# Stacked attention scores: one VectorE reduction in place of a ScalarE copy and a VectorE add, and the first parts of the keys made by ScalarE

## The chip, the cores and the metric

The kernel runs on one core of a Trainium2 chip. The metric is the device time of one execution in microseconds (us). Two timed runs of the kernel before gave 1043.73 and 1044.98 us, with a median of 1044.36. About 2% (21 us) of it is what counts as a difference here.

## The reference

The program is a linear attention, and behind it a mixture of experts that takes every token through all four experts. There are 32 heads of width 64 over 576 tokens, and 2304 tokens for the experts:

```
proj = x @ w_phi                      # x = q or k; w_phi is 64 x 128
proj = proj - max(|proj|) per row
phi  = concat(exp(proj), exp(-proj))  # 256 features
num  = phi(q) @ (phi(k).T @ v)
den  = phi(q) @ sum(phi(k)) + 1e-6
x    = num / den                      # heads side by side: 2304 x 512
out  = sum over e of p[:, e] * (relu(x @ w1[e]) @ w2[e])
```

All arrays are fp32. The kernel multiplies in a rounded fp32 format, and where that would cost accuracy it splits an operand into a first part ("hi": the value rounded) and a second part ("lo": the value minus the first part), and adds up products of the parts.

## The kernel before, in words

The attention is worked off in 16 **pairs** of heads, numbered 0 to 15 here. A pair has 576 tokens, laid out as 5 tiles of 128 for the keys (the last one half empty) and 4 tiles for the queries. They are taken in chunks: k 0 and k 1 have two tiles each, k 2 has one; q 0 and q 1 have two each.

From pair 4 on the scores are **stacked** (STACKED = 4). The 64 rows of a head's keys fill 64 partitions with their first parts, and the other 64 partitions hold their second parts; the weights `wst` hold the first parts of `w_phi` in columns 0 to 127 and the second parts in columns 128 to 255. One matmul of 128 x 256 (line 195) then leaves for each token two blocks of 128 columns whose sum is the score. A tile of two heads fills one PSUM tile of 512 columns. `proj_add` (lines 215 to 226) sums the blocks: ScalarE copies the second block from PSUM into the SBUF tile `d` (L225), then VectorE adds the first block to it (L226). `proj_sub` follows on VectorE: the maximum of the absolute values (L236) and its subtraction (L240). Then ScalarE takes the exponentials, TensorE transposes the queries' scores, and products follow.

`split_pair` (lines 165 to 183) makes those parts of the keys (`kst`) and queries (`qst`). `round_to` makes the first part on the engine that the tables HI_ENG0 (pairs 0 to 3) and HI_ENG (pairs 4 to 15) name, by a letter for the keys and one for the queries: v is VectorE (L160), a is ScalarE (L162), g is GpSimd (L158). The second part is always a subtraction on GpSimd (L181).

From pair 4 on the experts' matmuls on the first 512 tokens (L606, L570, `first_units`) are woven into the attention's. The order of everything is written by hand: STAGES gives each step of a pair a due time, 16 steps of a clock after the pair before, and a queue of steps is run down in the order of their due times (`run_until`). So the program order is fixed when the kernel is built, each engine works its own instructions strictly in that order, and they wait for each other only by semaphores. An instruction that waits holds up all that stand behind it on its engine.

Three PSUM tiles (`ps_att`, bufs=3) go round among the scores (`proj`), the transposed queries (`dT`) and the products (`num`). A matmul into such a tile waits until the reader of the tile three before it is through. Of `num`, the copies to `nd` are made by VectorE for the first head of the first 256 columns (L299) and by ScalarE for the rest (L301). They belong to the pair before the one whose keys are just being scored.

Of the kernel before, what the change touches and what calls it, by code (L numbers as in the profile page):

```python
# [13 lines left out]
AF = mybir.ActivationFunctionType  # L14
ALU = mybir.AluOpType
AX = mybir.AxisListType
# [4 lines left out]
def kernel(  # L21
# [16 lines left out]
    nc = tc.nc  # L38
# [3 lines left out]
    NF = w_phi.shape[1]  # L42
# [19 lines left out]


    COPY_ENG, COPY_ENG0 = "vvaaaa", "vaaaaa"
    LO_ENG, LO_ENG0, HI_ENG, HI_ENG0 = "vgg", "vgv", "vg", "ag"

    XA_START, XA_GAP, XA_LATE, XA_LOAD = 11, 0.7, 3.7, 1.5
    FETCH = (12, 28, 40, 46)
# [147 lines left out]
    def proj_add(i, what, c):  # L216

        s = pairs[i]
        if i < STACKED:
            return  # L220
        d = s.d[what, c] = ap_.tile([P, 512], F32, name="d", tag="d", bufs=3)
        for j, ps in enumerate(s.ps.pop((what, c))):
            a = ps.rearrange("p (h s f) -> p h s f", s=2, f=NF)
            dv = d[:, j * 256 : (j + 1) * 256].rearrange("p (h f) -> p h f", f=NF)
            nc.scalar.activation(dv, a[:, :, 1], AF.Copy)  # L225
            nc.vector.tensor_tensor(dv, a[:, :, 0], dv, op=ALU.add)  # L226

    def proj_sub(i, what, c):

# [199 lines left out]
    def x_store(i):  # L429
# [10 lines left out]
        (-7.5, split_pair, ("k",)),  # L440
        (-1.9, split_pair, ("q",)),
        (-0.3, proj, ("k", 0)), (0.1, proj_add, ("k", 0)), (0.6, proj_sub, ("k", 0)), (2.7, k_exp, (0,)),
        (7.2, k_kv, (0,)),
        (2.1, proj, ("k", 1)), (2.1, proj_add, ("k", 1)), (2.1, proj_sub, ("k", 1)), (3.9, k_exp, (1,)),
        (10, k_kv, (1,)),
        (2.8, proj, ("k", 2)), (3.1, proj_add, ("k", 2)), (3.4, proj_sub, ("k", 2)), (8.3, k_exp, (2,)),
        (12.2, k_kv, (2,)), (13, kv_hi, ()), (13.2, kv_lo, ()),
        (5.5, proj, ("q", 0)), (6.0, proj_add, ("q", 0)), (6.4, proj_sub, ("q", 0)), (8.4, q_tr, (0, 0)), (9.4, q_exp, (0, 0)),
# [488 lines left out]
```

## Time and profile before

| | |
|---|---|
| median of the timed runs | 1044.36 us (1043.73 to 1044.98) |
| the profiled execution, its own time | 1045.42 us |
| its span, first to last instruction | 1043.6 us |
| TensorE, matmuls busy | 977.1 us (94%) |
| VectorE busy | 725.0 us (69%) |
| ScalarE busy | 460.6 us (44%) |
| GpSimd busy | 584.8 us (56%) |
| `proj_add` of the stacked pairs runs from | 61.2 us to 396.5 us |

Busy time is the time in which an engine has an instruction under way; overlapping instructions are counted once, so the mean of one instruction times their count can be more than the group's busy time. The views below name engines PE (TensorE), DVE (VectorE), ACT (ScalarE) and POOL (GpSimd). Where an engine was idle ahead of an instruction, square brackets give the idle time and what ended it. A row with x2 or x4 merges so many instructions, and its second number is then the time from the first one's start to the last one's end.

### The profile page before, as it was taken

The page shows a single profiled execution, that of the slowest core. Times are in us where ns is not written, and L with a number is a line of the kernel's source. Part 1 is how long each engine was busy: PE and PEld are TensorE (multiplying, and loading weights), DVE is VectorE, ACT ScalarE, POOL GpSimd, SP SyncE. Part 2 cuts the span into 40 slices and gives each one's busy share as a digit, 9 for nine tenths or more (in the row PEclk, how much of TensorE's full clock was granted, in tenths as well). Part 3 has the DMA queues.
Part 4 walks back from the last instruction along what each step waited for, and adds up shares of the span by engine and source line. Part 5 has one row for each costly group of instructions (what it writes and reads, how often), then busy time and mean ns, then how long its engine had stood idle before and what let it go on. Part 6 is the DMA issues. An engine that isn't in the chain of part 4 may idle for free. (4 is left out here: it accounts for less than half of the span.)

```text
span 1043.6 us, 13596 instructions
## 1 busy us (share of the span) xinstructions
PE 977.1 (94%) x4923; PEld 833.9 (80%) x4923; DVE 725.0 (69%) x1110; ACT 460.6 (44%) x880; POOL 584.8 (56%) x439
## 2 busy tenths in 40 slices
PE   7977888999888889889999999999999999999998
PEld 6867777877777778667888888888878888888887
DVE  5567777776777676687667566666886767767764
ACT  4755554565455554344333333333343443443441
POOL 3645676775655663556445545544565556556551
PEclk9989999999999899999999999999999999999999
DMA  5422323332323213511212221121114122222211
GB/s 149 131 70 66 101 77 87 107 90 72 92 92 94 76 52 96 163 63 61 91 41 71 62 60 40 60 63 41 41 42 162 54 68 74 61 69 73 61 49 61
DMA packets 70610, 80.37 MB, mean 77 GB/s; under 512 B 34160, under 2 KB 36080, under 8 KB 70544
## 3 DMA queue, kind: packets, MB, share of 16 engines
q1 hardware_dynamic: 70544, 79.51, 25.5%
q8 instruction: 39, 0.64, 0.3%
q14 instruction: 27, 0.22, 0.1%
HBM read 72.00 MB, written 7.49 MB: 76 GB/s over the span
## 5 line engine op out<-in xcount | busy, mean ns | idle before, releaser
L580 DVE SCALAR_TENSOR_TENSOR out<-l,pr,out 128x512 f32<-128x512 f32 x270 | 200.4, 747 | 100.2 <-PE l L570 99.0
L570 PE MATMUL l<-w2hi,h_lo 128*128 128x512 f32 x576 | 229.9, 399 | 12.5 <-DVE out L580 12.5
L570 PE MATMUL l<-w2hi,h_hi 128*128 128x512 f32 x576 | 228.6, 397 | 0.0
L570 PE MATMUL l<-w2lo,h_hi 128*128 128x512 f32 x576 | 228.2, 396 | 0.0
L570 PEld LDWEIGHTS l<-w2hi,h_lo 128*128 128x128 f32 x576 | 109.7, 190 | 34.5 <-DVE out L580 17.0
L537 POOL TENSOR_TENSOR w1lo<-wraw,w1hi 128x512 fp32r<-128x512 f32 x64 | 79.7, 1265 | 96.5 <-ACT w1hi L529 58.6
L570 PEld LDWEIGHTS l<-w2hi,h_hi 128*128 128x128 f32 x576 | 109.6, 190 | 23.7
L500 POOL TENSOR_TENSOR w2lo<-wraw,w2hi 128x1024 fp32r<-128x1024 f32 x48 | 116.9, 2436 | 14.9 <-ACT w2hi L494 11.0
L570 PEld LDWEIGHTS l<-w2lo,h_hi 128*128 128x128 f32 x576 | 109.6, 190 | 17.6
L727 ACT ACTIVATE h_hi<-c 128x512 fp32r<-128x512 f32 (+1 forms) x96 | 55.0, 578 | 68.7 <-DVE c L724 67.7
L737 POOL TENSOR_TENSOR c<-u,s 128x512 f32<-128x512 f32 (+1 forms) x32 | 37.5, 1173 | 85.2 <-DVE u L724 85.2
L288 PEld LDWEIGHTS kv<-v,e 128*128 128x128 f32 x640 | 81.9, 200 | 3.7 <-issue 0.4
L181 POOL TENSOR_TENSOR kst<-kq,kst 64x640 fp32r<-64x640 f32 x24 | 42.8, 1783 | 66.2 <-issue 49.7
L288 PE MATMUL kv<-v,e 128*128 128x66 f32 x640 | 79.7, 279 | 0.0
L537 POOL TENSOR_TENSOR s_lo<-ws,s_hi 128x768 fp32r<-128x768 f32 x32 | 59.1, 1848 | 34.9 <-ACT s_hi L529 34.9
L753 ACT ACTIVATE c<-c 128x512 f32<-128x512 f32 (+1 forms) x32 | 18.5, 580 | 123.8 <-POOL c L737 123.8
L226 DVE TENSOR_TENSOR d<-proj,d 128x256 f32<-128x256 f32 x108 | 41.1, 417 | 46.0 <-ACT d L225 45.5
L240 DVE TENSOR_TENSOR d<-d,m 128x512 f32<-128x512 f32 (+1 forms) x60 | 66.5, 1108 | 2.1
L734 POOL TENSOR_TENSOR h_lo<-c,h_hi 128x512 fp32r<-128x512 f32 (+1 forms) x32 | 37.5, 1173 | 40.2 <-ACT h_hi L727 40.2
L494 ACT ACTIVATE w2hi<-wraw 128x1024 fp32r<-128x1024 f32 x48 | 50.6, 1053 | 13.7 <-PE l L570 13.2
L606 PE MATMUL l<-x_hi,w1lo 128*128 128x512 f32 x128 | 53.7, 419 | 0.0
L529 ACT ACTIVATE s_hi<-ws 128x768 fp32r<-128x768 f32 x32 | 27.1, 847 | 59.4 <-DVE ws L513 59.4
(156 smaller groups left out, 2291.3 us busy)
## 6 DMA issues: line engine op xcount, KB each, us to landing
wraw<-in_w_dram SPq DMA_DIRECT2D x96, 512.0 KB
kq<-in_kq_dram SPq DMA_DIRECT2D x31, 256.0 KB
rb<-rec_d SPq DMA_DIRECT2D x32, 144.0 KB
out_dram<-out SPq DMA_DIRECT2D x18, 256.0 KB
v<-in_v_dram SPq DMA_DIRECT2D x32, 128.0 KB
xd<-rb SPq DMA_DIRECT2D x8, 288.0 KB
xr<-xd SPq DMA_DIRECT2D x2, 768.0 KB
kq<-in_kq_dram SPq DMA_DIRECT2D x32, 32.0 KB
```

The lines of the kernel that those rows point to most:

```text
L181: nc.gpsimd.tensor_tensor(st[o, h], raw[r, sl], st[r, h].bitcast(F32), op=ALU.subtract)
L226: nc.vector.tensor_tensor(dv, a[:, :, 0], dv, op=ALU.add)
L240: nc.vector.tensor_tensor(d[:, :n].rearrange("p (g f) -> p g f", f=NF), psv, m[:, :g].unsqueeze(2).to_broadcast([P, g, NF]), op=ALU.subtract,)
L288: nc.tensor.matmul(s.kv[:, n * KW : (n + 1) * KW], lhsT=e[:, e0 : e0 + NF], rhs=s.v[:, t, h * KW : (h + 1) * KW], start=(c == 0 and j == 0 ...
L494: nc.scalar.activation(hi, raw, AF.Copy)
L500: nc.gpsimd.tensor_tensor(lo, raw, hi.bitcast(F32), op=ALU.subtract)
L537: nc.gpsimd.tensor_tensor(dst, src, hi.bitcast(F32), op=ALU.subtract)
L570: nc.tensor.matmul(ps, lhsT=l[:, f, j * P : (j + 1) * P], rhs=r[:, f, :], start=(f == 0 and k == 0), stop=(f == 1 and k == 2),)
L580: nc.vector.scalar_tensor_tensor(o, ps, p, o, op0=ALU.mult, op1=ALU.add)
L606: nc.tensor.matmul(banks[n, f], lhsT=l[:, ksl], rhs=r[:, k, :], start=(k == 0 and j == 0), stop=(k == NP - 1 and j == 2),)
L727: nc.scalar.activation(h[b][0][:, f, :nt], src, AF.Relu)
L734: nc.gpsimd.tensor_tensor(dst, src, hi.bitcast(F32), op=ALU.subtract)
```

## The change

In `proj_add` the copy and the addition give way to one VectorE instruction for each tile: a `tensor_reduce` that reads all 512 columns of the PSUM tile, viewed so that the two addends of a score stand innermost (they lie 128 columns apart), and writes their 256 sums to `d`. ScalarE has no part in it any more. And in HI_ENG the letter for the keys goes from v to a, so that ScalarE makes the first parts of the keys of pairs 4 to 15.

```diff
-    LO_ENG, LO_ENG0, HI_ENG, HI_ENG0 = "vgg", "vgv", "vg", "ag"
+    LO_ENG, LO_ENG0, HI_ENG, HI_ENG0 = "vgg", "vgv", "ag", "ag"
...
         for j, ps in enumerate(s.ps.pop((what, c))):
-            a = ps.rearrange("p (h s f) -> p h s f", s=2, f=NF)
+            a = ps.rearrange("p (h s f) -> p h f s", s=2, f=NF)
             dv = d[:, j * 256 : (j + 1) * 256].rearrange("p (h f) -> p h f", f=NF)
-            nc.scalar.activation(dv, a[:, :, 1], AF.Copy)
-            nc.vector.tensor_tensor(dv, a[:, :, 0], dv, op=ALU.add)
+            nc.vector.tensor_reduce(dv, a, axis=AX.X, op=ALU.add)
```

The changed file is one line shorter, so behind `proj_add` its line numbers are one lower. On TensorE, GpSimd and SyncE the instructions and their order stay as they were. On VectorE, 108 additions become 108 reductions in the same places, and 24 casts go. On ScalarE 108 copies go and 24 casts come.

The first place is VectorE on the keys of pair 9, from the first sum to the copy `nd` that ScalarE's next copies wait for. Before:

```order
L226 TENSOR_TENSOR d<-proj,d 128x256 x2
L236 TENSOR_REDUCE m<-d 128x4
L240 TENSOR_TENSOR d<-d,m 128x512
L580 SCALAR_TENSOR_TENSOR out_86<-l_2087,pr,out_86 128x512
L226 TENSOR_TENSOR d<-proj,d 128x256 x2
L236 TENSOR_REDUCE m<-d 128x4
L240 TENSOR_TENSOR d<-d,m 128x512
L226 TENSOR_TENSOR d<-proj,d 128x256
L236 TENSOR_REDUCE m<-d 128x2
L240 TENSOR_TENSOR d<-d,m 128x256
L299 TENSOR_SCALAR nd<-num,eps 128x256
```

Now:

```order
L225 TENSOR_REDUCE d<-proj 128x256 x2
L235 TENSOR_REDUCE m<-d 128x4
L239 TENSOR_TENSOR d<-d,m 128x512
L579 SCALAR_TENSOR_TENSOR out_86<-l_2040,pr,out_86 128x512
L225 TENSOR_REDUCE d<-proj 128x256 x2
L235 TENSOR_REDUCE m<-d 128x4
L239 TENSOR_TENSOR d<-d,m 128x512
L225 TENSOR_REDUCE d<-proj 128x256
L235 TENSOR_REDUCE m<-d 128x2
L239 TENSOR_TENSOR d<-d,m 128x256
L298 TENSOR_SCALAR nd<-num,eps 128x256
```

The five sums stand where they stood; each is now a reduction of 512 columns that reads PSUM alone.

The second place is ScalarE at the same time, from the last rounding of the exponentials of pair 8 (`ehi`) to its copy `nd`. Before:

```order
L258 ACTIVATE ehi<-e 128x640
L225 ACTIVATE d<-proj 128x256 x4
L494 ACTIVATE w2hi<-wraw 128x1024
L253 ACTIVATE e_2133<-d 128x4x128
L254 ACTIVATE e_2133<-d 128x4x128
L225 ACTIVATE d<-proj 128x256
L301 ACTIVATE nd<-num,eps 128x256
```

Now:

```order
L257 ACTIVATE ehi<-e 128x640
L493 ACTIVATE w2hi<-wraw 128x1024
L252 ACTIVATE e_2084<-d 128x4x128
L253 ACTIVATE e_2084<-d 128x4x128
L300 ACTIVATE nd<-num,eps 128x256
```

The five copies `d`, which stood behind `ehi`, are gone, and VectorE's sums no longer have ScalarE's queue ahead of them.

The third place is the cast of the keys of pair 10, before on VectorE, behind the sums of the last queries of pair 9:

```order
L226 TENSOR_TENSOR d<-proj,d 128x256 x2
L593 SCALAR_TENSOR_TENSOR h_lo<-l_2181,h_hi 128x512
L160 CAST kst<-kq 64x640 x2
L580 SCALAR_TENSOR_TENSOR out_86<-l_2255,pr,out_86 128x512
L236 TENSOR_REDUCE m<-d 128x4
```

and now on ScalarE, behind `h_hi`, ahead of the exponentials of pair 9's first queries:

```order
L622 ACTIVATE h_hi<-l_2131 128x512
L162 ACTIVATE kst<-kq 64x640 x2
L493 ACTIVATE w1hi<-wraw 128x1024
L252 ACTIVATE e<-dT 128x512
L253 ACTIVATE e<-dT 128x512
```

The cast has changed engines, and two instructions of 64 x 640 now stand ahead of `e` on ScalarE.

## Rows read from the trace of the kernel before

**Rows 1.** The page's first part: busy us, share of the span, instructions.

```profile
PE 977.1 (94%) x4923; PEld 833.9 (80%) x4923; DVE 725.0 (69%) x1110; ACT 460.6 (44%) x880; POOL 584.8 (56%) x439
```

**Rows 2.** Stretches of 14 us: length, busy us by engine, clock, DMA; sum.

```profile
200.00:214.00 14.00, 11.95 (x70) 9.99 (x68) 12.14 (x21) 8.99 (x21) 9.41 (x8) 1.00 0.37 108
214.00:228.00 14.00, 14.00 (x88) 12.32 (x87) 10.24 (x16) 7.56 (x16) 10.53 (x8) 1.00 0.24 60
...
sum 336.00, PE 294.74 PEld 251.51 DVE 242.13 ACT 181.20 POOL 206.78; mean PE 12.28 PEld 10.48 DVE 10.09 ACT 7.55 POOL 8.62
```

**Rows 3.** Waits from 60 to 400, TensorE, VectorE: us, times, longest.

```profile
PE proj L195 <- ACT nd L301: 12.0, 9, 2.1
PE proj L195 <- DVE d L226: 11.1, 16, 2.1
PE num L363 <- ACT nd L301: 9.4, 9, 3.2
...
DVE d L226 <- ACT d L225: 45.5, 30, 4.4
```

**Rows 4.** Groups by form, VectorE, ScalarE: count, busy us, mean ns, idle.

```profile
L240 DVE TENSOR_TENSOR d<-d,m 128x512 f32<-128x512 f32 x48 | 59.4, 1237 | 1.7
L226 DVE TENSOR_TENSOR d<-proj,d 128x256 f32<-128x256 f32 x108 | 41.1, 417 | 46.0 <-ACT d L225 45.5 <-PE l L570 0.5
...
L160 DVE CAST kst<-kq 64x640 fp32r<-64x640 f32 x24 | 12.1, 503 | 0.4
L240 DVE TENSOR_TENSOR d<-proj,m 128x512 f32<-128x512 f32 x16 | 11.1, 692 | 1.1
...
L236 DVE TENSOR_REDUCE m<-proj 128x4 f32<-128x512 f32 x16 | 11.0, 689 | 6.7 <-PE proj L211 6.6
...
L236 DVE TENSOR_REDUCE m<-proj 128x2 f32<-128x256 f32 x4 | 1.7, 422 | 0.6 <-PE proj L211 0.6
...
L856 DVE TENSOR_REDUCE prs<-pr 128x18 f32<-128x72 f32 x1 | 0.2, 217 | 0.0
...
L225 ACT ACTIVATE d<-proj 128x256 f32<-128x256 f32 x108 | 36.4, 381 | 21.9 <-PE proj L195 21.7
...
L162 ACT ACTIVATE kst<-kq 128x640 fp32r<-128x640 f32 x3 | 2.2, 737 | 0.1
```

**Rows 5.** VectorE by time, pair 9: start, us, line, idle before, releaser.

```profile
200.14 0.75 DVE L580 SCALAR_TENSOR_TENSOR out<-l,pr,out 128x512 f32<-128x512 f32 x1 [0.43 <-PE l L570]
201.21 0.76 DVE L226 TENSOR_TENSOR d<-proj,d 128x256 f32<-128x256 f32 x2 [0.32 <-ACT d L225]
...
208.47 0.48 DVE L299 TENSOR_SCALAR nd<-num,eps 128x256 f32<-128x256 f32 x1
```

**Rows 6.** ScalarE in order of time, pair 9.

```profile
208.98 0.47 ACT L301 ACTIVATE nd<-num,eps 128x256 f32<-128x256 f32 x1 [3.19 <-DVE nd L299]
```

**Rows 7.** TensorE in order of time, pair 9.

```profile
198.77 0.64 PE L195 MATMUL proj<-wst,kst 128*128 128x256 f32 x4
...
209.50 0.51 PE L195 MATMUL proj<-wst,qst 128*128 128x256 f32 x2 [0.96 <-ACT nd L301]
```

**Rows 8.** VectorE in order of time, pair 10.

```profile
226.73 0.21 DVE L393 RECIPROCAL rec<-den 128x9 f32<-128x9 f32 x1
229.25 0.76 DVE L226 TENSOR_TENSOR d<-proj,d 128x256 f32<-128x256 f32 x2 [2.31 <-ACT d L225]
...
236.60 0.47 DVE L299 TENSOR_SCALAR nd<-num,eps 128x256 f32<-128x256 f32 x1
```

**Rows 9.** TensorE in order of time, pair 10.

```profile
225.86 0.63 PE L195 MATMUL proj<-wst,kst 128*128 128x256 f32 x4
...
229.73 0.50 PE L195 MATMUL proj<-wst,kst 128*128 128x256 f32 x2 [0.93 <-DVE d L226]
...
237.63 0.50 PE L195 MATMUL proj<-wst,qst 128*128 128x256 f32 x2 [1.50 <-ACT nd L301]
```

**Rows 10.** GpSimd in order of time, ahead of pair 10.

```profile
218.60 3.44 POOL L181 TENSOR_TENSOR kst<-kq,kst 64x640 fp32r<-64x640 f32 x2 [3.17 <-issue]
```

## The prediction

> **What bounds the kernel now.** I start from the page's busy times: TensorE has matmuls under way in 94% of the span [rows 1], so a change can give back only time in which TensorE waits. The change touches the stretch of the stacked pairs, some 336 us of the span, so the next view is the engines' busy time there in stretches of 14 us. A pair takes about two of them, and they alternate [rows 2]: in the half in which a pair's keys are scored (200 to 214 us) VectorE is busy for 12.14 us of 14 and TensorE leaves 2.05 us idle; in the other half (214 to 228) TensorE has no gap and VectorE has 3.8 us to spare. Over the 336 us TensorE is idle for 336 - 294.74 = 41.3 us. The view of the waits says for what [rows 3]: 11.1 us for the additions of `proj_add` to give a PSUM tile back, 12.0 + 9.4 us for ScalarE's copies `nd`. Both hang on VectorE: the ScalarE copy of pair 9 at 208.98 sat idle for 3.19 us for VectorE's own `nd` [rows 6], which stands at the end of the VectorE chain of the keys' scores, at 208.47 [rows 5], and TensorE's next scores waited 0.96 us for that [rows 7]. So the question is when that chain starts and how long it is. The same view shows what may shorten it: VectorE sat for 45.5 us, in 30 waits, ahead of its additions until ScalarE's copies came [rows 3].
>
> **The change, part by part.**
>
> *The sums.* 108 additions of 417 ns and 108 copies of 381 ns [rows 4] go; 108 reductions of 512 columns come. No row shows such a reduction (pairs of columns 128 apart, from PSUM). The nearest is the maximum over 512 columns of a PSUM tile, 689 ns, and 422 ns over 256 [rows 4]: 267 ns for 256 columns, 1.04 ns a column. A penalty for many small groups would show in L856, with 18 groups of four: by the same slope 72 columns should take 422 - 184 x 1.04 = 230 ns, and it took 217 [rows 4]. Going by columns read, I take 689 ns, so +272 ns for each tile and +29.4 us of VectorE work in all. The lower end is the addition's 417 ns, if the work went by sums written; the upper end is a second read time for each column, 689 + 512 x 1.04 = 1222 ns, since every row here reads columns that lie side by side and excludes no price for a jump. I take the value near the lower end because rows of the same operation, from the same memory, with as many columns, give it.
>
> [...]
>
> *The casts.* 24 casts of 503 ns leave VectorE, -12.1 us [rows 4]. They stand behind the last queries' sums, in the half where VectorE has slack, so I count nothing for it. On ScalarE I take 737 ns, from its three casts of 640 columns on 128 partitions [rows 4], some +17.7 us against -36.4 us for the copies that go; it is busy for 7.56 us of that half's 14 [rows 2], which hides the casts. Behind the cast hangs GpSimd's subtraction `kst`: in pair 10 it ran from 218.60 to 222.04, after 3.17 us of idle time [rows 10], and TensorE first read it at 225.86 [rows 9]. That is 3.8 us of cover, against two casts of 1.5 us together; the cast may also come earlier, as it no longer stands behind a VectorE queue. SyncE's and GpSimd's orders do not change, no DMA is moved, and the new wait of the reductions, for a free `d`, falls on readers that are done before the scores come.
>
> *The start of the chain.* Without the copy, the first sum waits only for TensorE and for VectorE itself. Pair 9 is the worst case. TensorE was through with the two tiles at 198.77 + 0.64 = 199.41 [rows 7], VectorE came free at 200.14 + 0.75 = 200.89, and the additions began at 201.21 [rows 5]: 0.32 us are won. Pair 10 is the good case: scores done at 226.49 [rows 9], VectorE free at 226.94, additions at 229.25 [rows 8]: 2.30 us are won.
>
> *The length of the chain.* Two additions take 0.76 us [rows 5], two reductions by the same overlap 2 x 0.689 - 0.07 = 1.31: +0.55. The keys have two chunks of two tiles and one of one: +0.55 + 0.55 + 0.27 = +1.37 us up to `nd`.
>
> *The sum.* In pair 9 `nd` comes 1.37 - 0.32 = 1.05 us later, and TensorE, which waited for it, loses 1.05 us. In pair 10 it comes 2.30 - 1.37 = 0.93 us earlier; TensorE, which waited 0.93 us for the first sum and 1.50 us for `nd` [rows 9], can use it. What the second half does to it is nothing: TensorE is full there. The queries' sums gain by the missing copy about what they lose (two reductions after the scores instead of copy, then two additions). Twelve pairs between these ends give -11.2 to +12.6 us. The idle time ahead of all additions, 45.5 us [rows 3], against 29.4 us more work says that good and bad cases are mixed; I take the middle, +0.06 us a pair, +0.7 us in all. So the change moves 29 us onto an engine that is nearly full where it counts and takes away a handoff that cost it as much: **no difference that can be measured**. The profiled execution took 1045.42 us (span 1043.6 and 1.8 around it), 1.06 above the median of the timed runs. 1045.4 + 0.7 is 1046.1, by the median 1045.1; I say 1046.
>
> **The rivals.**
>
> *Slower: the jump is paid.* If a column that does not lie beside the last one costs a second read time, the reduction takes 1222 ns. The five tiles of the keys then add 5 x 0.533 = 2.67 us to the chain, so TensorE loses 3.7 us in pair 9 and 1.7 us in pair 10, 2.7 in the middle, 33 us for twelve pairs: 1079 us. It decides at about 0.34 us more than 689 ns a tile (5 x 12 x 0.34 = 21 us). [...] Against it: the row of 689 ns reads one column in 1.04 ns and shows no sign of the memory being the limit, but it reads side by side. Chance 0.19.
>
> *Faster: the chain also gets shorter.* The subtraction L240 takes 1237 ns where both operands are in SBUF and 692 ns where one is in PSUM [rows 4]; GpSimd works beside it for 8.62 us of every 14 [rows 2]. If ScalarE's earlier casts let GpSimd run its `kst` in its 3.17 us of idle time [rows 10], less of its work falls on the chain. If that wins half of the 0.545 us on two subtractions a pair, 12 x 2 x 0.27 = 6.5 us come off: 1039 us. With pair 10's case in most pairs besides (-11 us) it is 1028, and only with all the 0.545 us on top under 1024. Against it: GpSimd's next steps wait for ScalarE's exponentials of the pair, which do not come earlier. Chance 0.14, of which 0.05 below 1023.
>
> *The cast comes late.* If ScalarE reaches the cast so late that GpSimd's `kst` ends after 225.86, TensorE loses what goes over 3.8 us, in each pair; 2 us over would be 24 us, 1070. ScalarE stands idle for 6.4 us of that half, so I give it 0.02.
>
> That the change doesn't do what it says is excluded by the program order: the 108 reductions and the casts stand where the text puts them.
>
> **How the numbers follow.** The forecast, no measurable difference, has 0.65 and its own range is 1034 to 1058, the two ends of the sum. The faster rival has 0.14, the paid jump 0.19, the late cast 0.02. Two per cent, about what a measurement of this kernel can tell from no change, are 21 us: 1023.5 and 1065.2. Below lies 0.05. Above lie the paid jump and the late cast with 0.20, some of it nearer and some beyond 1079. Within lies 0.75. A range of 1032 to 1077 holds the forecast's own range (about 0.6 of all cases), two thirds of the faster rival and under half of the slower ones, some 0.8 together.
>
> **What would show it.** In the profile of the changed kernel the group of the reductions should read 690 ns; 950 or more means the paid jump, under 500 that it goes by sums written. VectorE's idle time for ScalarE ahead of the sums should be gone, and in its place stand waits for TensorE's scores. The chain from the first sum of pair 9 to its `nd`, 7.26 us before [rows 5], should take 8.6. TensorE's waits for the sums should stay near 11 us and those for `nd` near 21; if these fall to half, the faster rival is at work. ScalarE's casts should take 740 ns, and TensorE's waits for `kst` should stay small beside these. The prediction is wrong if the stretch of the stacked pairs changes its length by more than 13 us, whatever the reductions take.

## The result, and the profile after

Two timed runs of the changed kernel gave 1031.02 and 1032.16 us, a median of **1031.59 us** against 1044.36: a ratio of 0.9878 (95% interval 0.9835 to 0.9920). Six later executions gave 0.9843 (0.9811 to 0.9875). So it is some 13 to 16 us faster: a gain that is clear of the noise, and smaller than the 2% that the prediction set as the bound. The forecast was 1046 us; the time lies 0.4 us below the range of 1032 to 1077.

The profiled execution took 1031.02 us, its span is 1029.2 us and the mean granted clock of TensorE 0.986 (before: 1043.6 us, 0.976). The page's first part, which answers to [rows 1]:

```profile
PE 966.5 (94%) x4923; PEld 825.1 (80%) x4923; DVE 737.1 (72%) x1086; ACT 446.0 (43%) x796; POOL 575.2 (56%) x439
```

TensorE runs the same 4923 matmuls, but has them under way for 10.6 us less. Its idle time (span less busy time) went from 1043.6 - 977.1 = 66.5 us to 1029.2 - 966.5 = 62.7 us, by 3.8. So of 14.4 us of span about three quarters came from matmuls that ran faster, and one quarter from waits.

The groups by form, VectorE and ScalarE (count, busy us, mean ns, idle time before), which answer to [rows 4]:

```profile
L225 DVE TENSOR_REDUCE d<-proj 128x256 f32<-128x512 f32 x108 | 69.4, 678 | 7.7 <-PE proj L195 5.4 <-ACT kst L162 2.0
L239 DVE TENSOR_TENSOR d<-d,m 128x512 f32<-128x512 f32 x48 | 56.8, 1184 | 1.7
...
L235 DVE TENSOR_REDUCE m<-d 128x4 f32<-128x512 f32 x48 | 32.8, 683 | 1.2
...
L162 ACT ACTIVATE kst<-kq 64x640 fp32r<-64x640 f32 x24 | 17.7, 736 | 0.6
```

The reduction takes 678 ns, as the 689 of the forecast had it, and no more than the 683 ns of L235, which reads 512 columns that lie side by side in SBUF (688 ns where L235 reads PSUM): the jump of 128 columns cost nothing here. The casts took 736 ns (737 forecast). The 45.5 us in which VectorE sat idle for ScalarE's copies are gone; 2.0 us of waits for ScalarE's cast `kst` have come. But the subtraction, which the change did not touch, went from 1237 to 1184 ns.

The waits from 60 to 400 us (total us, times, longest), which answer to [rows 3], and those of GpSimd ahead of the second parts of the keys:

```profile
POOL kst L181 <- ACT kst L162: 20.0, 3, 10.1
...
POOL kst L181 <- issue: 14.2, 6, 5.1
...
PE proj L195 <- ACT nd L300: 12.7, 11, 2.0
...
PE proj L195 <- DVE d L225: 7.0, 11, 1.7
...
PE num L362 <- DVE d L225: 5.6, 5, 2.6
...
PE num L362 <- ACT nd L300: 3.3, 5, 1.1
```

TensorE's waits for `nd` fell from 21.4 to 16.0 us and those of `proj` for the sums from 11.1 to 7.0; a wait of 5.6 us of the products `num` for VectorE's sums is new. GpSimd's two rows in the kernel before, of the same view:

```profile
POOL kst L181 <- issue: 49.7, 9, 11.3
...
POOL kst L181 <- DVE kst L160: 15.6, 2, 8.5
```

GpSimd waited 65.3 us ahead of `kst` before, and 34.2 now (the row that says "issue" names no releaser). It gets to that work earlier in the pair: in the mean of pairs 5 to 15 its first `kst` starts 11.34 us ahead of VectorE's first sum, where it was 10.65 before. What that has to do with VectorE is seen in pair 9, VectorE in order of time, which answers to [rows 5] (start, duration):

```profile
194.03 1.27 DVE L225 TENSOR_REDUCE d<-proj 128x256 f32<-128x512 f32 x2
195.34 0.69 DVE L235 TENSOR_REDUCE m<-d 128x4 f32<-128x512 f32 x1
196.06 1.02 DVE L239 TENSOR_TENSOR d<-d,m 128x512 f32<-128x512 f32 x1
...
199.69 0.69 DVE L239 TENSOR_TENSOR d<-d,m 128x512 f32<-128x512 f32 x1
...
201.82 0.48 DVE L298 TENSOR_SCALAR nd<-num,eps 128x256 f32<-128x256 f32 x1
```

and GpSimd beside it:

```profile
194.94 3.54 POOL L265 TENSOR_TENSOR elo<-e,ehi 128x640 fp32r<-128x640 f32 x2
```

The same of the kernel before, VectorE's two subtractions and GpSimd's `elo`:

```profile
202.72 1.09 DVE L240 TENSOR_TENSOR d<-d,m 128x512 f32<-128x512 f32 x1
...
205.89 1.41 DVE L240 TENSOR_TENSOR d<-d,m 128x512 f32<-128x512 f32 x1
```

```profile
203.22 3.54 POOL L266 TENSOR_TENSOR elo<-e,ehi 128x640 fp32r<-128x640 f32 x2
```

Before, `elo` ran until 206.76, beside the second subtraction, which took 1.41 us. After, it was done at 198.48, before the second one began, and that took 0.69. From the first sum to `nd` the chain takes 201.82 - 194.03 = 7.79 us, against 7.26 before and 8.6 in the forecast: the sums added 0.51 + 0.53 + 0.27 = 1.31 us as priced, and the two subtractions gave 2.50 - 1.71 = 0.79 back. Read off in the same way for the eleven pairs 5 to 15 (in pair 4 no `nd` of VectorE stands behind the chain, though the forecast reckoned with twelve), the chain's mean went from 7.90 to 8.68 us (+0.78, forecast +1.37). That of its two 128 x 512 subtractions together went from 2.60 to 2.12 us, and its subtraction of 128 x 256 from 0.61 to 0.42. The queries' subtractions, which stand outside the chain, went the other way, from 2.43 to 2.65 us a pair, so that the mean of all 48 hides most of it. A subtraction beside which GpSimd did nothing took 0.69 us in every case of both traces; the others took 0.69 to 2.75.

Not every pair won. In pair 10, the forecast's good case, VectorE answers to [rows 8] with

```profile
222.15 1.22 DVE L225 TENSOR_REDUCE d<-proj 128x256 f32<-128x512 f32 x2
...
226.77 2.70 DVE L239 TENSOR_TENSOR d<-d,m 128x512 f32<-128x512 f32 x1
...
231.51 0.48 DVE L298 TENSOR_SCALAR nd<-num,eps 128x256 f32<-128x256 f32 x1
```

and GpSimd had this beside it:

```profile
226.54 2.38 POOL L499 TENSOR_TENSOR w2lo<-wraw,w2hi 128x1024 fp32r<-128x1024 f32 x1
```

The sums started without a wait, as forecast, but the chain took 9.36 us, where it had taken 7.35 in [rows 8]: one subtraction fell on GpSimd's split of a weight, and cost 2 us. What got shorter is the mean of the keys' subtractions, not that of each pair.

Where the matmuls became faster is seen in windows of the kernel before, in pair 10, just behind the two waits for `nd` (us; busy us by engine; granted clock; DMA):

```profile
236.00:238.00 2.00, 0.51 (x5) 0.37 (x4) 1.97 (x4) 0.89 (x2) 0.84 (x2) 1.00 0.00 0
238.00:240.00 2.00, 0.90 (x6) 0.41 (x4) 1.01 (x2) 1.74 (x5) 0.00 (x0) 0.94 0.32 122
240.00:242.00 2.00, 2.00 (x7) 2.00 (x8) 1.93 (x5) 1.44 (x4) 0.00 (x0) 0.50 0.08 31
242.00:244.00 2.00, 2.00 (x12) 1.72 (x12) 0.40 (x1) 1.20 (x3) 0.00 (x0) 0.70 0.14 10
```

TensorE was busy for 0.51 and then 0.90 us of 2, and behind that its granted clock stood at 0.50. The same matmul at that clock and, some 3 us later, at a clock of 1.00, TensorE in order of time:

```profile
242.14 0.63 PE L570 MATMUL l<-w2lo,h_hi 128*128 128x512 f32 x1
...
245.57 0.39 PE L570 MATMUL l<-w2lo,h_hi 128*128 128x512 f32 x1
```

A mean clock of 0.976 over 1043.6 us, if it is made of the levels 1.00 and 0.50 alone, means 2 x 0.024 x 1043.6 = 50 us at the lower one; 0.986 over 1029.2 us is 29. Matmuls of this size started 0.42 us apart at 0.50 and 0.23 apart at 1.00, so about half of the time at the lower level is lost: half of the 21 us between the kernels is 10.6, as much as TensorE's busy time lost. By this estimate the waits cost twice: once as idle time, and once as slow matmuls behind them.

### The profile page after: what moved, and what is told of

Its sections match the earlier page's. It is cut to its first block, busy times and chain, and to the rows that moved or that the text cites. A ratio compares the mean times of both kernels' runs of the same rounds, so it can differ in the third digit from the quotient of the medians.

```text
span 1029.2 us, 13480 instructions
## 1 busy us (share of the span) xinstructions
PE 966.5 (94%) x4923; PEld 825.1 (80%) x4923; DVE 737.1 (72%) x1086; ACT 446.0 (43%) x796; POOL 575.2 (56%) x439
## 5 line engine op out<-in xcount | busy, mean ns | idle before, releaser
L569 PE MATMUL l<-w2hi,h_lo 128*128 128x512 f32 x576 | 229.1, 398 | 13.0 <-DVE out L579 12.6
L225 DVE TENSOR_REDUCE d<-proj 128x256 f32<-128x512 f32 x108 | 69.4, 678 | 7.7 <-PE proj L195 5.4
L239 DVE TENSOR_TENSOR d<-d,m 128x512 f32<-128x512 f32 (+1 forms) x60 | 61.9, 1032 | 2.1
L181 POOL TENSOR_TENSOR kst<-kq,kst 64x640 fp32r<-64x640 f32 x24 | 38.0, 1585 | 36.5 <-ACT kst L162 20.0
L592 DVE SCALAR_TENSOR_TENSOR h_lo<-l,h_hi 128x512 fp32r<-128x512 f32 x32 | 22.0, 689 | 45.4 <-ACT h_hi L622 45.3
L499 POOL TENSOR_TENSOR w1lo<-wraw,w1hi 128x1024 fp32r<-128x1024 f32 x16 | 39.9, 2491 | 26.2 <-ACT w1hi L493 25.9
```

Source lines behind the costliest of these rows:

```text
L181: nc.gpsimd.tensor_tensor(st[o, h], raw[r, sl], st[r, h].bitcast(F32), op=ALU.subtract)
L225: nc.vector.tensor_reduce(dv, a, axis=AX.X, op=ALU.add)
L239: nc.vector.tensor_tensor(d[:, :n].rearrange("p (g f) -> p g f", f=NF), psv, m[:, :g].unsqueeze(2).to_broadcast([P, g, NF]), op=ALU.subtract,)
L499: nc.gpsimd.tensor_tensor(lo, raw, hi.bitcast(F32), op=ALU.subtract)
L569: nc.tensor.matmul(ps, lhsT=l[:, f, j * P : (j + 1) * P], rhs=r[:, f, :], start=(f == 0 and k == 0), stop=(f == 1 and k == 2),)
```

## The experiments

All ratios are to runs of the kernel before on the same chip, with 95% intervals. The theory after the result: the reduction by itself is worth about nothing, as forecast; the gain comes by the cast's move, in that GpSimd's reading falls less on VectorE's subtractions, and TensorE's clock adds to what is won. The rivals: the cast's move saves VectorE's time; ScalarE's relief is what pays; GpSimd's own results, coming earlier, are what pays.

**Each half alone.** From the changed kernel, and from the one before:

```diff
 # e1_sum_only: the changed kernel
-    ... HI_ENG, HI_ENG0 = "vgg", "vgv", "ag", "ag"
+    ... HI_ENG, HI_ENG0 = "vgg", "vgv", "vg", "ag"
 # e2_cast_only: the kernel before, the other way round
```

> The reduction alone, the casts of the keys stay on VectorE. If the gain of the change (1044.4 to 1031.6 us) is the reduction's, this reads 1030 to 1036 us, with fewer half-clock stretches of TensorE between 60 and 400 us than before. If the gain is the casts' (GpSimd's kst earlier, VectorE relieved of 12 us), it reads 1042 to 1050.

> The casts alone on ScalarE, copy and addition as before. If the gain is the reduction's: 1041 to 1047 us. If it is the casts': 1030 to 1036. If both are needed, this one and the run of the reduction alone both stay above 1038.

The sums alone gave 1.0038 (1.0007 to 1.0069), the cast alone 0.9951 (0.9933 to 0.9969). Neither is the 0.9843 of both: with the sums in place the cast is worth 2.0% (1.6% by the first two runs, 0.9878), without them 0.5%. The sums' 1053.59 us lie above the 1042 to 1050 of their expectation; the cast's 1042.84 fit "both are needed". With the cast alone VectorE's sums still sat idle for ScalarE's copies, nearly as long as before:

```profile
DVE d L226 <- ACT d L225: 42.6, 30, 4.4
```

The profiled execution of the sums alone was the longest of its ten (1058.09 us, median 1053.59). Its page, its subtraction, and the waits for and of GpSimd from 60 to 400 us:

```profile
PE 984.2 (93%) x4923; PEld 841.7 (80%) x4923; DVE 759.5 (72%) x1110; ACT 428.8 (41%) x772; POOL 585.6 (55%) x439
```

```profile
L239 DVE TENSOR_TENSOR d<-d,m 128x512 f32<-128x512 f32 x48 | 65.3, 1360 | 1.7
```

```profile
POOL kst L181 <- issue: 51.5, 9, 14.6
...
POOL kst L181 <- DVE kst L160: 15.6, 2, 8.8
...
PE num L362 <- POOL elo L265: 0.8, 1, 0.8
...
PE proj L195 <- POOL kst L181: 0.2, 1, 0.2
```

GpSimd waits 67.1 us ahead of `kst` here, as before the change, and the two subtractions of a chain take 3.01 us in the mean, against 2.60 before the change and 2.12 with the cast moved. The cast stands behind VectorE's longer queue here: the first `kst` starts 9.05 us ahead of the pair's first sum, later than before the change (10.65). So the sums by themselves make the stretching worse. But TensorE waits for GpSimd's own results for 1.0 us in all, so these are not late.

**TensorE's clock alone.** Into the waits of the kernel before went matmuls that nobody reads, 6 ahead of the queries' second tile and 4 ahead of the last `num` (they write the PSUM tile `kv`, which a pair takes earlier for that; those lines are not shown):

```diff
+    def fill(s, n):
+        for _ in range(n):
+            nc.tensor.matmul(s.kv[:, 0:256], lhsT=wst[:, 0:P], rhs=wst, start=True, stop=True, ...)
```

> The kernel before, with ten more matmuls of 128x256 in each stacked pair that nobody reads: six ahead of the query scores that wait for nd, four ahead of the last product of the pair before. They stand in the waits, so the waits for VectorE and ScalarE keep their cause. Theory 1 (most of the gain is TensorE's clock): the half-clock stretches between 120 and 365 us go, TensorE's other matmuls take some 8 us less, the surplus of the fillers where there is no wait costs some 3 to 6 us: 1037 to 1042. Theory 2 (the gain is shorter waits, the clock only follows): the waits do not shrink and the fillers cost time: 1046 to 1052.

> The changed kernel with the ten unread matmuls in each stacked pair. In the changed kernel's profile TensorE still ran some 24 us at half clock up to the end of the attention. If the fillers take most of that away, TensorE's other matmuls get 8 us shorter and the fillers cost 3 to 6 us: 1024 to 1031. If the clock has no more to give: 1034 to 1040.

The kernel before became 0.9906 (0.9877 to 0.9936), with a mean clock of 0.983 to 0.993 in its four runs (0.993 in the profiled one, the fastest) against 0.972 to 0.980 beside it, though it does more work. Its page counts the 120 added matmuls, and TensorE is busy for less time than before [rows 1]:

```profile
PE 975.2 (94%) x5043; PEld 835.4 (81%) x5043; DVE 725.4 (70%) x1110; ACT 460.4 (45%) x880; POOL 584.9 (57%) x439
```

The changed kernel with the same filling gave 0.9817 (0.9779 to 0.9854), inside the interval of the changed kernel itself (0.9811 to 0.9875): a further gain is not shown.

**VectorE's time, or ScalarE's.** The changed kernel with 24 casts of the keys that nobody reads on VectorE, and with 108 copies of 128 x 256 that nobody reads on ScalarE, ahead of the reductions:

```diff
 # e6_vector_casts_back, behind the cast of the keys
+            if what == "k":
+                nc.vector.tensor_copy(kjunk[r], raw[r, sl])
 # e7_scalar_load_back, ahead of the reduction
+            nc.scalar.activation(junk, wbd, AF.Copy)
```

> The changed kernel once more, beside the next three. Two runs gave 1031.6 us, a ratio of 0.988 to before. If that was a lucky draw of TensorE's half-clock stretches, the ratio moves to 0.99 or above; if the change has its gain in most executions, it stays at 0.980 to 0.989.

> The changed kernel, whose casts of the keys stay on ScalarE, with 24 casts of the same size on VectorE in their old places whose result nobody reads. Theory V (the cast matters by VectorE's time, as the reductions fill that engine): 1042 to 1054 us, like the reduction alone. Theory G (the cast matters because GpSimd's kst starts from ScalarE's queue instead of VectorE's): 1028 to 1036, like the change.

> The changed kernel with 108 copies of 128x256 on ScalarE in the places of the old ones that wait for nothing and that nobody reads. If the change gains by taking 36 us of work off ScalarE: 1038 to 1046 us. If ScalarE's work had cover and only the handoff from ScalarE to VectorE mattered: 1030 to 1036.

Beside the 0.9843 of the changed kernel the casts on VectorE gave 0.9902 (0.9872 to 0.9932) and the copies on ScalarE 0.9944 (0.9923 to 0.9965). The casts took 1366 ns each there, nearly three times the 503 of [rows 4], so that VectorE's time got more than its due, and still only 0.6% came back: 1037.67 us, between the ranges of theories V and G. The trace shows what stretched them, here in pair 13, VectorE and GpSimd:

```profile
303.18 2.66 DVE L183 CAST kjunk<-kq 64x640 fp32r<-64x640 f32 x1
```

```profile
303.12 2.37 POOL L502 TENSOR_TENSOR w2lo<-wraw,w2hi 128x1024 fp32r<-128x1024 f32 x1
```

The cast ended at 305.84, 0.35 us after GpSimd's instruction. So did all 21 of the 24 casts that began while GpSimd worked on operands in SBUF (0.34 to 0.35 us); the other three took 0.47 to 0.49 us.

ScalarE's load took back 1.0%; with it the subtraction was 1293 ns instead of 1184. Its 1041.19 us lie in the range that its expectation gave to ScalarE's 36 us of work. But the sums alone took that work off ScalarE as well and gained nothing, so the relief by itself does not pay; and the load delays the cast that ScalarE now makes (11.81 us ahead of the first sum, against 12.24 in the changed kernel). So VectorE's time is the lesser part of the 2%, and the part of ScalarE's load is not separated from that of the cast.

**GpSimd held up.** The changed kernel with three memsets of 128 x 1024 on GpSimd, behind the cast of the keys and ahead of `kst`:

```diff
+            if what == "k" and h == 0:
+                nc.scalar.activation(gj[:, 0:1], eps[:, 0:1], AF.Copy)
+                for _ in range(3):
+                    nc.gpsimd.memset(gj, 0.0)
```

> The changed kernel with GpSimd held up by three memsets of 128x1024 ahead of its kst of each stacked pair, behind the cast; they read nothing. Theory G (the early cast pays because GpSimd is through with more of its reading when VectorE's chain of the keys' sums runs, and so stretches its two subtractions of 128x512 less): the two together go from 2.1 us a pair back to 2.6 to 3.0 and the time to 1038 to 1048 us. Theory V (only VectorE's own relief pays): the time stays at 1029 to 1034.

1.0030 (1.0011 to 1.0050): the whole gain is gone, and the two subtractions took 2.86 us a chain. The 1050.86 us are above even the 1038 to 1048 of theory G. But it is no clean proof. TensorE's idle time rose by 1045.8 - 972.9 - 62.7 = 10.2 us, and this row of its waits is over half of that:

```profile
PE proj L200 <- POOL kst L186: 6.2, 4, 2.1
```

So GpSimd's late results could be the cause as well as its reading. The same trace shows what GpSimd does to a subtraction; VectorE, in order of time:

```profile
175.48 2.68 DVE L244 TENSOR_TENSOR d<-d,m 128x512 f32<-128x512 f32 x1
...
193.19 0.69 DVE L244 TENSOR_TENSOR d<-d,m 128x512 f32<-128x512 f32 x1
```

and GpSimd:

```profile
175.22 2.39 POOL L504 TENSOR_TENSOR w1lo<-wraw,w1hi 128x1024 fp32r<-128x1024 f32 x1
...
192.60 2.98 POOL L185 MEMSET gj<- 128x1024 f32 x3 [3.77 <-ACT gj L183]
```

Beside GpSimd's subtraction of a weight, with both operands in SBUF, VectorE's ended 0.55 us after that one (178.16 and 177.61), as if it had got on only then. In this trace and those of the kernels before and after, 46 of VectorE's subtractions began while GpSimd subtracted 128 x 1024, and 45 of them ended 0.54 to 0.55 us after it (the other one began with 0.01 us of it left). In the three of this trace that lay wholly beside memsets it took 0.69. It holds the other way too: the 22 such subtractions of GpSimd that began during one of VectorE's took 2.49 to 2.84 us instead of 2.4, and ended 2.21 to 2.26 us after it.

**GpSimd made quiet.** That gave the test of the open question. `elo` of the stacked pairs and the weights' `w1lo` and `w2lo` of the attention subtract 8 columns only, and memsets hold GpSimd for the rest of their time (the kernel leaves these second parts out), once with the cast moved and once without:

```diff
+    def quiet(lo, e, hi, sizes):           # sizes: 640, 640, 384 or 1024, 1024, 512
+        nc.gpsimd.tensor_tensor(lo[:, 0:8], e[:, 0:8], hi[:, 0:8].bitcast(F32), op=ALU.subtract)
+        for n in sizes:
+            nc.gpsimd.memset(lo[:, 8:n].bitcast(F32), 0.0)
```

> The changed kernel, with GpSimd's subtractions elo of the stacked pairs and those of the experts' weights that fall into the attention cut down to their first 8 columns; memsets of the same columns follow, so that GpSimd is held about as long (1.6 and 2.4 us) but reads almost nothing. The second parts of the exponentials and of those weights are thus left out. Theory A (the gain of the cast's move is carried by the stretching of VectorE's subtractions by GpSimd's reading): the two 128x512 subtractions of a chain go from 2.14 us together to near 1.4, 12 pairs by 0.75 us are 9 us, and with TensorE's clock some 0.9 to 1.5% come off the changed kernel's 0.984: a ratio of 0.970 to 0.977. Theory B (the gain is that GpSimd's own results come earlier, and the stretching is only seen beside it): GpSimd is no earlier here, so the ratio stays at 0.981 to 0.987.

> The reductions alone (the casts of the keys stay on VectorE), with the same quiet GpSimd and the same parts left out. Theory A: the two subtractions go from 3.01 us a chain to near 1.4, so the same 1.6 us a pair (19 us) come off 1.004: a ratio of 0.970 to 0.985, within 1% of the changed kernel made quiet. Theory B: the casts still hold up GpSimd's kst, so a gap of about 2% to the changed kernel made quiet stays, and the ratio is 0.995 or more.

With the cast moved: 0.9776 (0.9734 to 0.9818). Without: 0.9792 (0.9752 to 0.9832). The 2.0% between the two became 0.2%, less than the intervals tell apart. The subtraction and GpSimd's waits from 60 to 400 us, with the cast moved:

```profile
L239 DVE TENSOR_TENSOR d<-d,m 128x512 f32<-128x512 f32 x48 | 37.1, 774 | 1.7
```

```profile
POOL kst L181 <- issue: 18.8, 6, 5.1
...
POOL kst L181 <- ACT kst L162: 9.9, 2, 5.0
```

and without:

```profile
L239 DVE TENSOR_TENSOR d<-d,m 128x512 f32<-128x512 f32 x48 | 39.0, 813 | 1.7
```

```profile
POOL kst L181 <- issue: 44.0, 10, 8.3
...
POOL kst L181 <- DVE kst L160: 7.5, 1, 7.5
```

GpSimd still comes to `kst` later without the cast's move (8.75 us ahead of the first sum against 11.09, with 51.5 us of waits against 28.7), but as it hardly reads beside the subtractions any more, that costs nothing that can be measured. It was not its results that came earlier: without the move it is through with `elo` 6.47 us after the pair's first sum, later than the 5.71 us of the sums alone that were not made quiet, and yet the time is 2.5% shorter. So the gain is carried by the stretching, and GpSimd's own results were early enough all along. The runs take the stretching off all of VectorE's instructions beside these reads, not off the two subtractions of the chain alone. The kernel before was not made quiet, so what the reductions are worth without any stretching is not shown. The theory's size was met for the kernel without the cast's move (0.970 to 0.985) and missed by a hair for the other (0.970 to 0.977).

**The chain made longer on purpose.** The changed kernel with each reduction of the keys done twice (60 more):

```diff
             nc.vector.tensor_reduce(dv, a, axis=AX.X, op=ALU.add)
+            if what == "k":
+                nc.vector.tensor_reduce(dv, a, axis=AX.X, op=ALU.add)
```

> The changed kernel with every reduction of a key tile made twice, so VectorE's chain from the first sum to nd gets 5 x 0.65 = 3.3 us longer in each pair. If a pair's TensorE waits follow the chain one for one: 12 x 3.3 = 39 us and some lost clock, 1066 to 1085 us. If VectorE has cover there: under 1050.

1.0312 (1.0272 to 1.0353), 4.8% or some 49 us above the changed kernel and inside the expected 1066 to 1085, where 60 x 0.691 = 41 us were added. Its page:

```profile
PE 987.1 (92%) x4923; PEld 839.4 (78%) x4923; DVE 776.4 (72%) x1146; ACT 446.4 (41%) x796; POOL 572.1 (53%) x439
```

With a span of 1076.8 us TensorE is idle for 89.7 us, 27.0 more than in the changed kernel, and has the same matmuls under way for 20.6 us more. So TensorE's waits grew by two thirds of the 41 us that VectorE was given, and slower matmuls added three quarters as much again.

**A better version.** In both kernels the copy `nd` of the first head went from VectorE to ScalarE, out of the end of VectorE's chain:

```diff
-    COPY_ENG, COPY_ENG0 = "vvaaaa", "vaaaaa"
+    COPY_ENG, COPY_ENG0 = "vaaaaa", "vaaaaa"
```

> The changed kernel with the copy nd of the first head on ScalarE too in the stacked pairs, so that no copy nd stands behind VectorE's chain of the keys' sums. If TensorE's waits for nd come from the end of that chain, the 16 us of them mostly go and the clock stays full: 1015 to 1024 us. If ScalarE's own queue is as late (its exponentials ahead of nd wait for VectorE's first subtraction), the waits shrink by a third at most: 1026 to 1032.

> The kernel before with nd of the first head on ScalarE. If the end of VectorE's chain is what TensorE waited for, this gives about what it gave the changed kernel: 1028 to 1035 us. If it pays only with ScalarE's copies d gone, as they stand ahead of nd on that engine: 1038 to 1046.

> The version with nd on ScalarE (1018 us) and the ten unread matmuls a pair. TensorE's clock was full there for all but some 14 us, so the fillers have little to give back and mostly cost: 1020 to 1027 us. If most executions of that version did meet more half-clock stretches than its profile shows, it reads 1012 to 1018.

On the changed kernel **1018.33 us, 0.9735** (0.9694 to 0.9776), faster than both kernels; on the kernel before 0.9857 (0.9824 to 0.9891). The filling on top gave 0.9768 (0.9734 to 0.9802), no gain: the clock stood at 0.993 already in three of the four runs without it. The page and TensorE's waits of the best version:

```profile
PE 959.4 (94%) x4923; PEld 819.6 (81%) x4923; DVE 739.4 (73%) x1074; ACT 451.1 (44%) x808; POOL 576.3 (57%) x439
```

```profile
PE proj L195 <- DVE d L225: 7.0, 10, 1.7
...
PE num L362 <- DVE d L225: 6.4, 4, 2.6
...
PE num L362 <- ACT nd L300: 4.0, 5, 1.5
```

The 12.7 us of `proj` waiting for `nd` are gone, and the mean clock of the profiled execution is 0.993.

## Why the prediction was wrong

- **The sums: right.** 689 ns were taken, 678 measured, and the rival of the paid jump fell. That a jump costs a second read time for each column, the 1222 ns of that rival, was the author's estimate, and no run shows it: the reduction took 678 ns, against 688 over columns side by side in PSUM. By itself this half of the change came out at 1.0038, about what the forecast said of the whole; but that was in part luck, as the subtractions took longer in it (3.01 us a chain against 2.60), which the forecast did not have.
- **The casts: the step that failed.** "They stand behind the last queries' sums, in the half where VectorE has slack, so I count nothing for it." It asked whether the casts' time was hidden, and whether GpSimd's `kst` would come too late. The sum did not ask what GpSimd's earlier start would no longer collide with; that was left to a rival with a chance of 0.14. That earlier start was worth 2.0% once the sums were in place, and nothing measurable (0.2%) once GpSimd hardly read beside the subtractions.
- **The length of the chain: half right.** Of the +1.37 us the sums' part came as priced. The two subtractions of 128 x 512 gave 0.48 us a pair back and the one of 128 x 256 another 0.18; 0.14 us of idle time inside the chain came. That is the rival "faster: the chain also gets shorter", which had 0.14; it had the mechanism, and its size (half of 0.545 us on each of two subtractions). What was held against it, that GpSimd's next steps wait for ScalarE's exponentials, is there (9.7 us in six waits of `elo` for `ehi` in the changed kernel), but did not undo it. In the traces a subtraction took 0.69 us beside memsets and up to 2.75 beside GpSimd's subtractions, and the mean of the 108 reductions was 678 ns in the changed kernel and 680 with the sums alone and in both runs with GpSimd quiet. The forecast knew the two prices, 1237 and 692 ns, and took the first as fixed.
- **The sum: right for the waits, wrong for what they cost.** The idle time of TensorE fell by 3.8 us, well inside the forecast's -11.2 to +12.6. The start of the chain came as forecast too: ahead of the first sums of pairs 5 to 15 VectorE had been idle for 18.4 us in all, now for 0.3. But "TensorE loses 1.05 us" for a wait of 1.05 us left out the matmuls behind it: another 10.6 us came off the matmuls, which ran at a higher mean clock (0.986 against 0.976). So the term that the sum put at nothing, slower matmuls behind a wait, was the larger part of what changed. Filling the waits alone gave 0.9%, and the doubled sums cost 20.6 us of slower matmuls on top of 27.0 of waiting.
- **What would show it: mostly as written.** The waits for ScalarE ahead of the sums went but for 2.0 us, waits for the scores came (5.4 us), the casts took 736 ns. The sign that was named for the faster rival, waits that fall to half, was too strict: they fell by a quarter (21.4 to 16.0) to a third (11.1 to 7.0). The last sign came: from the first to the last instruction of `proj_add` the stacked pairs took 335.7 us before and 320.7 after, 15 us less, where more than 13 was to mean a wrong prediction.

What stays open is how the 2.0% divides between idle time and clock. The profiles of the two kernels differ by 9.1 us of idle time and 17.7 of busy time, but the profiled execution of the sums alone was its longest.

## What to carry to other kernels

When an instruction moves between engines, look at what the engine behind it will now run at another time, and which instructions on SBUF operands lie there: in this case a group whose mean was well above its shortest case (1237 against 690 ns) had such a neighbour, and moving the neighbour was worth 2.0%. Price a wait of the bounding engine with the clock behind it, from windows of the trace that show it lower after such waits (in the kernel before 0.50 behind those of pair 10, but 1.00 behind that of pair 9). And a half that is worth nothing alone can be what lets the other half pay, so run the halves apart before keeping or dropping one.

## What the runs showed of the hardware

- A VectorE reduction that adds pairs of fp32 columns 128 apart in PSUM (512 in, 256 out) took 678 ns, no more than one over 512 columns side by side (683 from SBUF, 688 from PSUM).
- VectorE's fp32 subtraction of 128 x 512 with both operands in SBUF took 0.69 us beside an idle GpSimd or its memsets. Where it began during GpSimd's subtraction of 128 x 1024 it ended 0.54 to 0.55 us after that, 45 times out of 46 in three traces, and took 0.70 to 2.75 us. GpSimd's was held up likewise when it began second: 2.49 to 2.84 us instead of 2.4, 22 times.
- 120 matmuls that nobody reads made a kernel 0.9% faster: TensorE's mean granted clock was 0.983 to 0.993 with them, 0.972 to 0.980 without.
- VectorE's cast of 64 x 640 took 0.47 to 0.49 us where GpSimd was idle at its start. Where it began while GpSimd worked on operands in SBUF it ended 0.34 to 0.35 us after GpSimd's instruction, 21 times out of 21, and took 0.52 to 2.66 us.
